# Mixing the tokens of each pair of heads in the space of the keys

## The chip, the core and the metric

The kernel runs on one core of a Trainium2 chip. A core has five engines with an instruction stream of their own: PE (TensorE, which multiplies matrices; its weight loads are listed apart as PEld), DVE (VectorE), ACT (ScalarE), POOL (GpSimd) and SP (SyncE, which issues the DMA transfers here). Engines wait for one another by semaphores. SBUF is the working memory of 128 partitions, PSUM the memory of eight banks into which PE writes. The metric is device time in microseconds; the shown runs of one kernel lie within 0.15% of one another, and this document calls a difference of under 0.2% (3.6 us) no change.

## The reference

Cut to what matters: an attention whose keys and values are averaged over 8 neighbouring tokens (576 tokens, 72 keys), a mixing of the tokens by two low-rank matrices U (576 x 32) and V (32 x 576), and two large feed-forward layers.

```python
# q, k, v: 8 batches, 8 heads, 576 tokens, 64 features
k_p = k.reshape(B, H, Sp, pool, D).mean(axis=3)      # 72 keys
v_p = v.reshape(B, H, Sp, pool, D).mean(axis=3)
scores = scale * q @ k_p.T;  attn = softmax(scores)   # 576 x 72 for each head
x = attn @ v_p                                        # then 8 x 576 x 512
h = x.transpose(0, 2, 1) @ U @ V                      # mixes the 576 tokens
u = x + h.transpose(0, 2, 1)
x = u + relu(u @ w_ch1) @ w_ch2                       # layer 1: 512 -> 2048 -> 512
# layer 2: layer norm, the same form, another pair of weights
```

## The kernel before, in words

Weights arrive as 64-bit floats and are decoded on the chip by integer operations on DVE (lines 564 to 593). Most products are made of two 32-bit pieces in the reduced format fp32r, a high part and the rest (`split`, line 519), so that one product of the reference becomes three matmuls: high by high, rest by high, high by rest. A few small ones are made in full fp32; the trace lists each of those as two records.

The attention runs over 32 pairs of heads, four pairs to a batch (`att_steps`, line 1019). For a pair P: load q, k, v; sum keys and values over 8 tokens (`att_prep`); scores of all 576 tokens against 2 x 72 keys, in five row tiles of 128 tokens, the last one overlapping (`att_s`, five fp32 matmuls of 144 columns); minimum, exponential, sum and division (`att_m`), which leaves the tile `sc` [128 tokens, 5, 144]; transposes of `sc` to key by token (`att_t`, eight of 128 tokens and two of 64); the product with the values (`att_av`), which leaves `xT` [128 features, 576 tokens].

Before the change, the four `xT` of a batch are then mixed at its end: `att_xt` transposes them back to token by feature (20 transposes), splits them (in the first two batches with an extra matmul against a negative identity, `split_ps`, line 533), `att_g` multiplies with U (ten matmuls of 512 columns; U stands in `ust` with its pieces side by side), `att_gs` cuts the product into pieces (`gs`), `att_vm` multiplies with V (eight matmuls of 288 columns) and adds to `xT` on DVE. Then `a_split` (first batch) or a trip through DRAM (`u_d`, `a_prep`) gives layer 1 its input.

Layer 1 runs in groups of 512 tokens (`a_l1`, 12 matmuls of 512 columns for each of 8 slices of weights, then `a_l2`). The group w-1 of layer 1 is interleaved with the attention of batch w, so that PE has its matmuls to do while the attention waits. The first batch has no such partner.

The order is made by a planner in the kernel file (`Order.schedule`, line 151): every operation has a cost for each engine that may do it, a priority that grows with the PE cost of what was written before it (shifted by biases), and buffers from rings; the planner gives each operation to an engine and emits each engine's stream in order of planned start. An engine then works its stream strictly in that order. The PSUM ring of the attention, `py`, has four banks handed out in turn.

The names and lines that the steps touch: `att_t` 849, `att_xt` 931, `att_g` 949, `att_gs` 961, `att_vm` 975, the order of steps 1028 to 1053, `setup_uv` (decodes U and V) 609, its place 1128.

Of the kernel before, what the change touches and what calls it, by code (L numbers as in the profile page):

```python
# [8 lines left out]
F32 = mybir.dt.float32  # L9
# [28 lines left out]
UT = [0, 128, 256, 384, 512]  # L38
# [363 lines left out]
class Kern:  # L402
    def __init__(self, nc, tc, aps):
# [129 lines left out]
    def split_ps(self, hi, lo, ps, src, n, m):  # L533

        nc, o = self.nc, self.o
        on = {ACT: c_act(n, True), DVE: c_dve(n)}
        part = lambda: src(ps.t)
        o.op({ACT: on[ACT]}, lambda e: copy(nc, e, hi(), part()), r=[ps], w=[hi.a])
        o.op(
            {PE: c_pe(n)},  # L540
            lambda e: e.matmul(part(), self.minus[:m, :m], hi(), start=False, stop=True, skip_group_check=True),
            r=[hi.a],
            w=[ps],
        )
        o.op(on, lambda e: copy(nc, e, lo(), part()), r=[ps], w=[lo.a])

# [62 lines left out]
    def setup_uv(self):  # L609
# [4 lines left out]
        def load(raw):  # L614
            o.op(
                {GP: 200},
                lambda e: e.memset(raw.t[64:, 4 * RANK : n].bitcast(I32), 0),
# [11 lines left out]
            o.op({SY: 450}, lambda e: e.dma_start(raw.t[:64, 4 * RANK : n], self.U[512:]), w=[(raw, 1)], size=16384)  # L629
# [5 lines left out]

        for c in (0, 1, 3):
# [14 lines left out]
        for z in range(2):  # L651
# [11 lines left out]
            x = self.staged(SH, load)  # L663
# [185 lines left out]
    def att_t(self, P, j):  # L849
# [24 lines left out]
        o.op({PE: cost}, mm, r=[sc], w=[ps])  # L874
        if P < LEAN_T:
# [55 lines left out]
    def att_xt(self, b, i):  # L931
        o = self.o
        n = 128 if i < 4 else 64
        ps, xh, xl = self.buf("py"), self.buf("xh"), self.buf("xl")
        xs = [self.xT[NP * b + p] for p in range(NP)]

        def mm(e):
            for p in range(NP):
                turn(e, ps.t[:n, p * 128 : p * 128 + 128], xs[p].t[:, UT[i] : UT[i] + n], self.ident, p == 0)

        o.op({PE: 4 * 110}, mm, r=xs, w=[ps])
        top = lambda t: t[:n]
        if NP * b < LEAN_X:
            self.split_ps(View(xh, None, top), View(xl, None, top), ps, top, DM, n)
        else:
            self.split(View(xh, None, top), View(xl, None, top), View(ps, None, top), DM, ps=True, hi_on=(ACT,))
        self.xhl[i] = (xh, xl, n)

    def att_g(self, b, i):
        if i == 0:  # L950
            self.pg = self.buf("py")
        pg = self.pg
        xh, xl, n = self.xhl[i]

        def mm(e):
            e.matmul(pg.t, self.ust.t[:n, i], xh.t[:n], start=(i == 0), stop=False)  # L956
            e.matmul(pg.t, self.ust.t[:n, i], xl.t[:n], start=False, stop=(i == 4))  # L957

        self.o.op({PE: c_pe(DM, 2)}, mm, r=[xh, xl, self.ust], w=[pg])

    def att_gs(self, b):
        nc, o = self.nc, self.o
        gr, gs, pg = self.buf("gr"), self.buf("gs"), self.pg
        o.op({ACT: c_act(DM, True)}, lambda e: copy(nc, e, gr.t, pg.t), r=[pg], w=[gr])
        o.op(
            {DVE: c_dve(DM) + 60},
# [697 lines left out]
```

## Time and profile before

| | us |
|---|---|
| median of 3 runs (lowest, highest) | 1775.42 (1773.33, 1775.81) |
| the profiled execution | 1774.35 |
| its span in the trace | 1772.6 |
| PE busy | 1738.5 (98%) |
| DVE busy | 973.2 (55%) |
| POOL, ACT busy | 745.9 (42%), 723.8 (41%) |

The span is what the trace covers; 1.75 us lie around it. Busy shares are means over stages that differ: up to about 93 us the attention of the first batch and the start of the second, then layer 1 interleaved with the other batches up to about 475 us, the rest of layer 1 to about 620 us, and layer 2.

### The profile page before, as it was taken

To read this page: it belongs to the slowest core of one execution; us is meant where nothing else is said; L and a number is where in the kernel's file an instruction comes from. 1 tells how busy PE (TensorE), PEld (TensorE's weight loads), DVE (VectorE), ACT (ScalarE), POOL (GpSimd) and SP (SyncE) were. 2 spreads that over 40 slices of the span, in tenths; PEclk is the share of its full clock that TensorE was granted. 3 is DMA by queue.
4 is the path that set the end of the run, shared out by engine and by line. 5 is a ranking of instruction groups with operands and counts; after the bars stand their busy time and mean duration, and the time that the engine had idled before them with its cause. 6 is when DMAs were issued, how large, how long until landed. Compare 5 with 4: busy or idle time off the path is not lost.

```text
span 1772.6 us, 26907 instructions
## 1 busy us (share of the span) xinstructions
PE 1738.5 (98%) x10156; PEld 1519.6 (86%) x10156; DVE 973.2 (55%) x1858; ACT 723.8 (41%) x1897; POOL 745.9 (42%) x638
## 2 busy tenths in 40 slices
PE   5899999999999999999999999999999999999998
PEld 4678888888888889999999988999999999899997
DVE  8998888888646354444445766553224633333333
ACT  5556556655632233333333443333333433223221
POOL 1233224222100066666666653333334455555654
PEclk8799999999999999999999999999999999999999
DMA  6555544654343153544444444332112423233222
GB/s 194 179 165 181 189 162 155 206 182 132 108 141 112 42 196 123 123 120 122 121 120 106 132 130 157 119 122 81 48 48 84 143 101 102 102 114 112 102 78 78
DMA packets 95251, 222.97 MB, mean 126 GB/s; under 512 B 14225, under 2 KB 14225, under 8 KB 89361
## 3 DMA queue, kind: packets, MB, share of 16 engines
q1 hardware_dynamic: 94976, 221.25, 39.4%
q8 instruction: 79, 1.29, 0.3%
q14 instruction: 52, 0.42, 0.1%
q10 hardware_dynamic: 144, 0.00, 0.0%
HBM read 152.00 MB, written 69.22 MB: 125 GB/s over the span
## 4 chain that ended last, share of the span: by engine, by line
PE 94%; DVE 4%; DMA 1%; ACT 0%; issue 0%; DVEq 0%; ACTq 0%
PE py L1387 33%; PE pa L1299 17%; PE pbc L1299 13%; PE pbc L1097 11%; PE pa L1069 10%; PE py L378 3%; PE py L792 2%; PE py L918 1%; PE py L919 1%; PE py L900 1%; PE py L956 1%; PE py L957 0%; PE py L981 0%; PE pbc L1522 0%; DMA wraw<-w_d 0%
## 5 line engine op out<-in xcount | busy, mean ns | idle before, releaser
L1387 PE MATMUL py<-hid,w2h 128*128 128x512 f32 x1728 | 541.2, 394 | 0.2 <-DVE hid L1327 0.2
L1387 PE MATMUL py<-hid,w2l 128*128 128x512 f32 x864 | 338.6, 392 | 0.0
L1299 PE MATMUL pa<-op,w1h 128*128 128x256 f32 x1728 | 326.2, 281 | 0.5 <-ACT s L383 0.3
L1299 PEld LDWEIGHTS pa<-op,w1h 128*128 128x128 f32 x1728 | 293.9, 188 | 37.0 <-DVE s L385 0.6
L528 POOL TENSOR_TENSOR op<-xraw,op 128x512 fp32r<-128x512 f32 x130 | 171.5, 1321 | 280.2 <-ACT op L383 275.7
L1357 DVE TENSOR_TENSOR pbc<-s,pbc 128x512 f32<-128x512 f32 x108 | 75.1, 696 | 390.2 <-PE pbc L1299 386.0
L1387 PEld LDWEIGHTS py<-hid,w2h 128*128 128x128 f32 x1728 | 273.5, 189 | 11.0 <-DVE hid L1327 0.5
L1299 PEld LDWEIGHTS pbc<-op,w1h 128*128 128x128 f32 x1296 | 220.7, 188 | 28.1
L1299 PE MATMUL pbc<-op,w1h 128*128 128x256 f32 x1296 | 244.3, 281 | 0.0
L1299 PE MATMUL pa<-op,w1l 128*128 128x256 f32 x864 | 242.6, 281 | 0.0
L1387 PEld LDWEIGHTS py<-hid,w2l 128*128 128x128 f32 x864 | 162.4, 188 | 36.7
L1097 PE MATMUL pbc<-op,wh 128*128 128x512 f32 x576 | 183.7, 400 | 0.0
L1069 PE MATMUL pa<-hid,wh 128*128 128x512 f32 x576 | 181.9, 397 | 0.0
L1299 PE MATMUL pbc<-op,w1l 128*128 128x256 f32 x648 | 181.8, 280 | 0.0
L1299 PEld LDWEIGHTS pa<-op,w1l 128*128 128x128 f32 x864 | 162.9, 189 | 0.0
L1327 DVE SCALAR_TENSOR_TENSOR hid<-pa,hid 128x512 fp32r<-128x512 f32 x108 | 74.5, 690 | 123.8 <-ACT hid L1321 123.6
L1321 ACT ACTIVATE hid<-pa 128x512 fp32r<-128x512 f32 x108 | 64.6, 598 | 188.5 <-PE pa L1299 184.2
L1321 ACT ACTIVATE hid<-pbc 128x512 fp32r<-128x512 f32 x108 | 64.6, 598 | 184.9 <-DVE pbc L1357 183.9
L1253 POOL TENSOR_TENSOR t<-xraw 128x512 f32<-128x512 f32 x52 | 67.8, 1303 | 138.3 <-DMA xraw<-n_d 80.8
L1069 PEld LDWEIGHTS pa<-hid,wh 128*128 128x128 f32 x576 | 104.9, 188 | 20.9 <-issue 0.4
L1299 PEld LDWEIGHTS pbc<-op,w1l 128*128 128x128 f32 x648 | 121.9, 188 | 0.0
L1097 PEld LDWEIGHTS pbc<-op,wh 128*128 128x128 f32 x576 | 103.1, 188 | 20.8 <-issue 2.2
(187 smaller groups left out, 2896.0 us busy)
## 6 DMA issues: line engine op xcount, KB each, us to landing
xraw<-n_d SPq DMA_DIRECT2D x18, 1024.0 KB
wraw<-wC SPq DMA_DIRECT2D x32, 512.0 KB
wraw<-wA SPq DMA_DIRECT2D x24, 512.0 KB
w_d<-wx SPq DMA_DIRECT2D x48, 256.0 KB
wraw<-w_d SPq DMA_DIRECT2D x48, 256.0 KB
k<-kT SPq DMA_DIRECT2D x32, 288.0 KB
q<-qT SPq DMA_DIRECT2D x32, 288.0 KB
v<-v SPq DMA_DIRECT2D x32, 288.0 KB
```

The costliest lines, as they stand in the source:

```text
L378: e.matmul(out, src, ident, start=first, stop=True, is_transpose=True, skip_group_check=True)
L528: lambda e: e.tensor_sub(lo(), src(), hi().bitcast(F32)),
L792: lambda e: e.matmul(ps.t[:, i : i + 2 * SP], q.t[:, QT[t] : QT[t] + 128], kbd.t.rearrange("p h n -> p (h n)"), start=True, stop=True, ski ...
L900: lambda e: e.matmul(ps.t[:, :SH], vs.t[:, w], ef.t[:, h, c], start=(h == 0), stop=(h == 1)),
L1069: e.matmul(ps.t, w.t[:, c], u.t, start=(i == 0), stop=(i == 3 * NCC - 1))
L1097: e.matmul(ps.t, w.t[:, c], x.t, start=(f == 0 and j == 0), stop=(f == NA - 1 and j == 2))
L1253: o.op(on, lambda e: e.tensor_sub(dst(), a(), c()), r=r, w=w)
L1299: e.matmul(bank.t[:, sl], w.t[:, self.WCOL[k], c], u.t[:, t], start=(first and i == 0), stop=(last and i == 5), skip_group_check=True,)
L1321: lambda e: e.activation(h.t[:, :TG], bank.t, AF.Relu),
L1327: lambda e: e.scalar_tensor_tensor(l.t[:, :TG], bank.t, 0.0, h.t[:, :TG].bitcast(F32), op0=ALU.max, op1=ALU.subtract),
L1357: o.op({DVE: c_dve(TG)}, lambda e: e.tensor_add(c.t, s.t, c.t), r=[s], w=[c])
L1387: e.matmul(y.t, w.t[:, i, c], x.t[:, :TG], start=(first and q == 0), stop=(last and q == 2))
```

## The change

The mixing is linear in the softmax weights, so the kernel applies U and V to them and not to the attention's result. For each pair, `att_u` multiplies the softmax weights (144 columns) with U; for pairs 0 to 7 in fp32 with a plain copy of U (`us`), for the others with the split pieces (`sh`, `sl`) in ten matmuls. `gs` is now 144 columns for a pair. `att_t` transposes `sc` as before and then adds `gs` times V into the same PSUM banks: two matmuls of 512 columns and two of 64. The evicted weights are the mixed ones; `att_av` then gives the mixed `xT` at once, and `att_out` stores it. `att_xt`, `att_g`, `att_vm` and `split_ps` are gone, all pairs have the same order of steps, and U and V are decoded right after the first pair's preparation (`first`), not in the middle of the first batch.

```diff
-        ring(att, "xT", [128, S], n=5)
-        ring(att, "xh", [128, DM], F32R, 2)
-        ring(att, "xl", [128, DM], F32R, 2)
-        ring(att, "gr", [128, DM], F32R)
-        ring(att, "gs", [128, DM], F32R)
+        ring(att, "xT", [128, S], n=3)
+        ring(att, "sh", [128, 5, 2 * SP], F32R)
+        ring(att, "sl", [128, 5, 2 * SP], F32R)
+        ring(att, "gr", [128, 2 * SP], F32R, 2)
+        ring(att, "gs", [128, 2 * SP], F32R, 2)
...
+        ring(att, "us", [128, 5, 128])
...
+        self.us = self.buf("us")
+        o.op({GP: 500}, lambda e: e.memset(self.us.t, 0.0), w=[self.us])
+        for c in (0, 1, 3):
...
+        gs = self.gs[P]
+        parts = [(j, slice(0, 512), slice(0, 512))] if j < 2 else [
+            (h, slice(h * 64, h * 64 + 64), slice(512, S)) for h in range(2)
+        ]
+
+        def add(e):
+            for h, a, k in parts:
+                e.matmul(
+                    ps.t[:SP, a], gs.t[:, h * SP : h * SP + SP], self.vst.t[:, k], start=False, stop=True,
+                    skip_group_check=True,
+                )
+
+        o.op({PE: c_pe(512) if j < 2 else 2 * 65}, add, r=[gs, self.vst], w=[ps])
...
+    def att_u(self, P):
+        nc, o = self.nc, self.o
+        sc, ps = self.sc[P], self.buf("py")
+        row = lambda t: slice(64 if t == 4 else 0, 128)
+        if P < LEAN_U:
+
+            def mm(e):
+                for t in range(5):
+                    r = row(t)
+                    e.matmul(ps.t[:, : 2 * SP], self.us.t[r, t], sc.t[r, t], start=(t == 0), stop=(t == 4))
+
+            o.op({PE: 5 * 200}, mm, r=[sc, self.us], w=[ps])
         else:
...
+            h, l = self.buf("sh"), self.buf("sl")
+            whole = lambda t: t
+            self.split(View(h, None, whole), View(l, None, whole), View(sc, None, whole), 10 * SP)
+
+            def mm(e):
+                for t in range(5):
+                    r = row(t)
+                    e.matmul(ps.t[:, : 2 * SP], self.ust.t[r, t], h.t[r, t], start=(t == 0), stop=False)
+                    e.matmul(ps.t[:, : 2 * SP], self.ust.t[r, t], l.t[r, t], start=False, stop=(t == 4))
+
+            o.op({PE: 10 * 75}, mm, r=[h, l, self.ust], w=[ps])
+        gr, gs = self.buf("gr"), self.buf("gs")
+        o.op({ACT: c_act(2 * SP, True)}, lambda e: copy(nc, e, gr.t, ps.t[:, : 2 * SP]), r=[ps], w=[gr])
...
-        first += [m(0)]
+        first += [m(0), lambda: self.att_u(0)]
...
-                seq += [M_, x[0], x[1], g[0], x[2], R_[0], g[1], x[3], g[2], x[4], g[3], g[4], gs]
-                seq += vm
+            seq = [S_[0], R_[2], S_[1], T_[0], S_[2], S_[3], T_[1], S_[4], T_[2], R_[1], M_, V_[0]]
+            seq += [V_[1], R_[0], V_[2], V_[3], out, U_]
```

Where the planner puts it shows at two places of the PE stream and one of the DVE stream. In the rows a name with its buffer number stands left of the arrow for what is written and right of it for what is read.

The first place is the PE stream from the end of the first batch's mixing to the first matmuls of layer 1 (`pa0<-hid0,wh00`). Before, first half of that stretch and its end:

```order
L981 MATMUL py3_249<-vstk0_189,gs0_187 128x288
L981 MATMUL py2_248<-vstk0_189,gs0_187 128x288
L981 MATMUL py0_246<-vstk0_189,gs0_187 128x288
L981 MATMUL py1_247<-vstk0_189,gs0_187 128x288
L792 MATMUL py3_249<-kbd1_154,q1_156 128x144 x2
L378 MATMUL py2_248<-ident_60,sc0_167 72x128 x4
L792 MATMUL py3_249<-kbd1_154,q1_156 128x144
L792 MATMUL py0_246<-kbd1_154,q1_156 128x144
L378 MATMUL py1_247<-ident_60,sc0_167 72x128 x4
L792 MATMUL py0_246<-kbd1_154,q1_156 128x144
L378 MATMUL py2_248<-ident_60,sc0_167 72x64 x2
L1069 MATMUL pa0_242<-hid0_209,wh00_220 128x512
```

Now, the same stretch, with the fifth pair's product with U (`py<-sc,us`), scores (`kbd,q`), transposes (`ident,sc`) and additions (`vstk,gs`):

```order
L948 MATMUL py1_246<-sc0_167,us0_187 128x144 x5
L787 MATMUL py3_248<-kbd1_154,q1_156 128x144 x2
L377 MATMUL py2_247<-ident_60,sc0_167 72x128 x4
L877 MATMUL py2_247<-vstk0_188,gs0_184 72x512
L787 MATMUL py3_248<-kbd1_154,q1_156 128x144
L787 MATMUL py0_245<-kbd1_154,q1_156 128x144
L377 MATMUL py1_246<-ident_60,sc0_167 72x128 x4
L877 MATMUL py1_246<-vstk0_188,gs0_184 72x512
L787 MATMUL py0_245<-kbd1_154,q1_156 128x144
L377 MATMUL py2_247<-ident_60,sc0_167 72x64 x2
L877 MATMUL py2_247<-vstk0_188,gs0_184 72x64 x2
L1049 MATMUL pa0_241<-hid0_208,wh00_219 128x512
```

The products of the batch's mixing (`vstk0,gs0` of 288 columns, and before them the transposes of `xT` and the products with `ust`) no longer stand ahead of layer 1; three additions of the fifth pair stand there, and layer 1 begins behind them.

The second place is the PE stream in the stretch where layer 1 and attention are interleaved. Before, the third batch's four products with V behind layer 1's matmuls (`pbc0<-op14,wh70`):

```order
L1097 MATMUL pbc0_244<-op14_207,wh70_234 128x512
L1097 MATMUL pbc0_244<-op15_208,wh70_234 128x512
L1097 MATMUL pbc0_244<-op14_207,wl70_235 128x512
L981 MATMUL py2_248<-vstk0_189,gs0_187 128x288
L981 MATMUL py0_246<-vstk0_189,gs0_187 128x288
L981 MATMUL py3_249<-vstk0_189,gs0_187 128x288
L981 MATMUL py1_247<-vstk0_189,gs0_187 128x288
L1097 MATMUL pbc1_245<-op0_193,wh00_220 128x512
```

Now the ninth pair's last products with U (`sh`, `sl`: high and rest of the softmax weights), then the tenth pair's scores, the ninth's transposes and first addition:

```order
L959 MATMUL py3_248<-sh0_180,ust0_186 128x144
L960 MATMUL py3_248<-sl0_181,ust0_186 128x144
L959 MATMUL py3_248<-sh0_180,ust0_186 128x144
L960 MATMUL py3_248<-sl0_181,ust0_186 128x144
L787 MATMUL py0_245<-kbd1_154,q1_156 128x144 x2
L377 MATMUL py2_247<-ident_60,sc0_167 72x128 x4
L787 MATMUL py0_245<-kbd1_154,q1_156 128x144
L787 MATMUL py1_246<-kbd1_154,q1_156 128x144
L877 MATMUL py2_247<-vstk0_188,gs0_184 72x512
L377 MATMUL py3_248<-ident_60,sc0_167 72x128 x4
L1077 MATMUL pbc0_243<-op8_200,wh40_227 128x512
```

Ten short products for each pair have come into the stream, each with a weight load of its own, and the first addition follows them behind five short groups.

The third place is the DVE stream just ahead of layer 1's first matmuls. Before, the pieces `gs0` of the first batch and the additions to `xT`:

```order
L593 SCALAR_TENSOR_TENSOR wx0_145<-wraw0_144,wx0_145 128x512
L967 SCALAR_TENSOR_TENSOR gs0_187<-gr0_186,neg_b_72,py1_247 128x512
L528 TENSOR_TENSOR wl40_229<-wx0_145,wh40_228 128x512
L988 TENSOR_TENSOR xT0_177<-xT0_177,py3_249 128x288
L988 TENSOR_TENSOR xT0_177<-xT0_177,py2_248 128x288
L988 TENSOR_TENSOR xT1_178<-xT1_178,py0_246 128x288
L385 CAST hid0_209<-xT0_177 128x512
L988 TENSOR_TENSOR xT1_178<-xT1_178,py1_247 128x288
L988 TENSOR_TENSOR xT2_179<-xT2_179,py3_249 128x288
L988 TENSOR_TENSOR xT2_179<-xT2_179,py2_248 128x288
L988 TENSOR_TENSOR xT3_180<-xT3_180,py0_246 128x288
```

Now the splits of the fourth pair's result (`hid6`, `hid7`), decoding (`wx0`, `at0`, `wt0`) and the fifth pair's `gs0`:

```order
L833 RECIPROCAL sm0_171<-sm0_171 128x10
L384 CAST hid6_214<-xT0_177 128x512
L837 TENSOR_TENSOR sc0_167<-sc0_167,sm0_171 128x720
L528 TENSOR_TENSOR hid7_215<-xT0_177,hid6_214 128x512
L564 TENSOR_SCALAR wt0_146<-wt0_146 128x512
L528 TENSOR_TENSOR wl00_220<-ax0_151,wh00_219 128x512
L571 SCALAR_TENSOR_TENSOR wx0_145<-wraw0_144,wt0_146 128x512
L579 SCALAR_TENSOR_TENSOR wx0_145<-wraw0_144,wx0_145 128x512
L554 TENSOR_SCALAR at0_152<-araw0_150 128x512
L967 SCALAR_TENSOR_TENSOR gs0_184<-gr0_182,neg_b_72,py1_246 128x144
```

The eight additions to `xT` are gone from DVE; splits that POOL and ACT made before, a piece `gs` for each pair and more of the weights' decoding stand in their place.

## Rows read from the trace of the kernel before

**Rows 1.** The page, part 1: engine, busy us (share), instructions.

```profile
PE 1738.5 (98%) x10156; PEld 1519.6 (86%) x10156; DVE 973.2 (55%) x1858; ACT 723.8 (41%) x1897; POOL 745.9 (42%) x638
```

**Rows 2.** Busy time by stretch: us, then each engine, PEclk, DMA.

```profile
0.00:20.00 20.00, 9.30 (x38) 7.72 (x39) 14.23 (x36) 10.36 (x49) 4.63 (x20) 1.00 0.67 210
20.00:48.00 28.00, 20.33 (x83) 15.17 (x83) 23.96 (x60) 15.52 (x71) 4.35 (x4) 0.69 0.58 182
48.00:72.00 24.00, 18.41 (x68) 13.49 (x67) 22.07 (x44) 12.72 (x31) 5.45 (x6) 0.65 0.54 186
72.00:93.00 21.00, 18.15 (x95) 14.53 (x94) 20.66 (x45) 13.72 (x64) 5.85 (x7) 1.00 0.47 147
93.00:475.00 382.00, 381.19 (x2013) 316.34 (x2012) 317.49 (x677) 229.85 (x824) 108.92 (x122) 1.00 0.53 170
...
620.00:1772.00 1152.00, 1146.09 (x7195) 1032.27 (x7194) 505.61 (x870) 398.35 (x775) 610.87 (x475) 1.00 0.36 111
```

**Rows 3.** Timeline of PE, first batch's mixing: start us, us, operation, count.

```profile
48.89 1.91 PE L378 MATMUL py<-ident,xT 128*128 128x128 f32 x8
...
60.24 0.50 PE L957 MATMUL py<-xl,ust 64*128 64x512 f32 x1 [0.43 <-ACT xl L383]
64.24 3.19 PE L981 MATMUL py<-vstk,gs 128*128 128x288 f32 x8 [3.50 <-DVE gs L967]
...
71.76 0.73 PE L1069 MATMUL pa<-hid,wh 128*128 128x512 f32 x2
```

**Rows 4.** Groups of DVE by form, 0 to 72 us: busy, mean ns.

```profile
L842 DVE TENSOR_TENSOR sc<-sc,sm 128x720 f32<-128x720 f32 x5 | 4.5, 900 | 0.0
...
L988 DVE TENSOR_TENSOR xT<-xT,py 128x288 f32<-128x288 f32 x8 | 3.1, 446 | 0.0
...
L967 DVE SCALAR_TENSOR_TENSOR gs<-gr,neg_b,py 128x512 fp32r<-128x512 f32 x1 | 0.7, 740 | 0.0
```

**Rows 5.** Timeline of PE in the third batch's mixing, saturated stretch.

```profile
173.22 1.03 PE L378 MATMUL py<-ident,xT 128*128 128x128 f32 x8
174.01 0.72 PE L1069 MATMUL pa<-hid,wh 128*128 128x512 f32 x2
174.57 0.40 PE L1069 MATMUL pa<-hid,wl 128*128 128x512 f32 x1
...
185.29 0.39 PE L1097 MATMUL pbc<-op,wl 128*128 128x512 f32 x1
185.61 0.50 PE L956 MATMUL py<-xh,ust 64*128 64x512 f32 x1
185.94 0.39 PE L957 MATMUL py<-xl,ust 64*128 64x512 f32 x1
186.27 0.73 PE L1097 MATMUL pbc<-op,wh 128*128 128x512 f32 x2
186.83 0.40 PE L1097 MATMUL pbc<-op,wl 128*128 128x512 f32 x1
...
189.12 0.68 PE L981 MATMUL py<-vstk,gs 128*128 128x288 f32 x4
189.64 0.63 PE L1097 MATMUL pbc<-op,wh 128*128 128x512 f32 x2
190.11 0.39 PE L1097 MATMUL pbc<-op,wl 128*128 128x512 f32 x1
```

**Rows 6.** Timeline of PE, the score products of the same stretch.

```profile
200.71 0.90 PE L792 MATMUL py<-kbd,q 128*128 128x144 f32 x6
201.35 0.73 PE L1097 MATMUL pbc<-op,wh 128*128 128x512 f32 x2
201.92 0.40 PE L1097 MATMUL pbc<-op,wl 128*128 128x512 f32 x1
```

**Rows 7.** Timeline of PE, products of one column, in the second layer.

```profile
697.34 0.95 PE L1522 MATMUL pbc<-few,lns 128*128 128x1 f32 x8
698.15 0.48 PE L1299 MATMUL pa<-op,w1h 128*128 128x256 f32 x2
```

More of the change, by code (lines that the diff above doesn't have):

```diff
@@ L531, in split @@
         )
[L533 to L545, printed above, removed]
     def decode(self, x, tmp, raw):
@@ L634, in u @@
             return t[:, :n].rearrange("p (i r) -> p i r", r=RANK)
+        self.us = self.buf("us")
+        o.op({GP: 500}, lambda e: e.memset(self.us.t, 0.0), w=[self.us])
+        for c in (0, 1, 3):
+            o.op(
+                {ACT: c_act(n), DVE: c_fast(n)},
+                lambda e, c=c: copy(nc, e, self.us.t[:, :, c * RANK : (c + 1) * RANK], u(x.t)),
+                r=[x],
+                w=[(self.us, c)],
+            )
         for c in (0, 1, 3):
@@ L661, in load @@
                     )
-            x = self.staged(SH, load)
+            x = self.staged(SH, load, 'aw'[z])
             o.op(
@@ L965, in att_gs @@
         o.op(
-            {DVE: c_dve(DM) + 60},
+            {DVE: c_dve(2 * SP) + 60},
             lambda e: e.scalar_tensor_tensor(
-                gs.t, gr.t.bitcast(F32), self.neg_b, pg.t, op0=ALU.mult, op1=ALU.add
+                gs.t, gr.t.bitcast(F32), self.neg_b, ps.t[:, : 2 * SP], op0=ALU.mult, op1=ALU.add
             ),
-            r=[gr, pg],
+            r=[gr, ps],
             w=[gs],
         )
-        self.gs = gs
-    def att_vm(self, b, half, c):
+        self.gs[P] = gs
@@ L976, in att_vm, with att_out @@
+    def att_out(self, P):
         o = self.o
-        x, gs, ps = self.xT[NP * b + c], self.gs, self.buf("py")
-        s = slice(half * SH, half * SH + SH)
-        o.op(
-            {PE: c_pe(SH)},
-            lambda e: e.matmul(
-                ps.t[:, :SH], gs.t[:, c * 128 : c * 128 + 128], self.vst.t[:, s], start=True, stop=True
-            ),
-            r=[gs, self.vst],
-            w=[ps],
-        )
-        keys = [(x, (h, half)) for h in range(2)]
-        o.op({DVE: c_dve(SH)}, lambda e: e.tensor_add(x.t[:, s], x.t[:, s], ps.t[:, :SH]), r=[ps], w=keys)
@@ L1028, in att_steps @@
         pv = lambda P: (lambda: self.att_prep_v(P))
-        first = [ld(0), pr(0), pv(0), ld(1)] + [s(0, t) for t in range(5)] + [pr(1), pv(1), ld(2)]
-        first += [m(0)]
+        first = [ld(0), pr(0), self.setup_uv, pv(0), ld(1)] + [s(0, t) for t in range(5)] + [pr(1), pv(1), ld(2)]
+        first += [m(0), lambda: self.att_u(0)]
         for P in range(B * NP):
             N = P + 1
-            last = P % NP == NP - 1
             S_ = [s(N, t) for t in range(5)] if N < B * NP else [None] * 5
             M_ = m(N) if N < B * NP else None
+            U_ = (lambda N=N: self.att_u(N)) if N < B * NP else None
             R_ = [ld(P + 3), pr(P + 2), pv(P + 2)] if P + 2 < B * NP else [None] * 3
@@ L1038, in att_steps @@
             V_ = [av(P, 0, 0), av(P, 1, 0), av(P, 0, 1), av(P, 1, 1)]
[L1039 to L1050 removed]
+            out = lambda P=P: self.att_out(P)
+            seq = [S_[0], R_[2], S_[1], T_[0], S_[2], S_[3], T_[1], S_[4], T_[2], R_[1], M_, V_[0]]
+            seq += [V_[1], R_[0], V_[2], V_[3], out, U_]
             if P == 0:
@@ L1127, in phase_a @@
         per = self.att_steps()
[L1128 to L1131 removed]
+        for st in per[0]:
             st()
```

72 lines of the change are left out of this document (15 added, 57 removed).

## The prediction

> **What bounds the kernel now.** I read the page's busy shares first: PE is busy for 98% of the span, no other engine for more than 55% [rows 1]. That is a mean, so next the busy time by stretch [rows 2]. From 93 to 475 us, where layer 1 and the attention are interleaved, PE is busy 381.2 of 382 us at a granted clock of 1.00: there every microsecond of PE work that is added or taken is a microsecond of the kernel. DVE has 64 us to spare in that stretch and ACT 152. The first 72 us are another matter: PE idles 5 to 11 us in each of three stretches, its clock is 0.69 and 0.65 of full speed in two of them (a mix of the 1.2 and 2.4 GHz levels, after idle gaps), and DVE is busy 60.3 of 72 us, 46.0 of the last 52. Third, the timeline of PE around the first batch's mixing [rows 3]: the transposes back begin at 48.89, the last product with U at 60.24, PE then waits 3.50 us for `gs`, multiplies with V at 64.24, and layer 1 begins at 71.76. So the change touches two things with different prices: the amount of PE work where PE is the bound, and the time at which layer 1 can begin.
>
> **PE work in the saturated stretch, taken away.** The third batch shows what a mixing costs there [rows 5]. Two products of 512 columns take 190.11 - 189.64 = 0.47 us, so 0.23 each. Eight transposes and two such products lie between 173.22 and 174.57: 1.35 - 0.46 = 0.89, so 0.11 for a transpose and 2.2 for twenty. The ten products with U are 2.3 us, and the last two of them, on 64 rows, cost more: from 185.52 (0.23 behind the start at 185.29) to 186.37 (0.46 ahead of 186.83) it is 0.85 us where two products elsewhere take 0.46. So a visit to 64 rows costs 0.39 extra, and U 2.7 in all. The four products with V take 190.11 - 0.46 - 189.12 = 0.53 us, so 0.13 each and 1.05 for eight. A batch's mixing is 2.2 + 2.7 + 1.05 = 5.95 us of PE. Seven batches lie behind the start of layer 1: 41.65, and the second batch has five products with the negative identity besides, 5 x 0.23 = 1.15. Taken away: 42.8 us.
>
> **PE work added.** At the start of layer 1 the fifth pair's additions are done (the order shows it), so 27 pairs are left. Each adds two products of 512 columns (0.46) and two of 64. The latter are not in the trace; products of one column take (698.15 - 697.34) / 8 = 0.10 each [rows 7], and I take that: 0.66 a pair, 17.8 us. Three pairs have the product with U in fp32, 144 columns with 128 x 128 weights, which is the form of the scores: six records take 201.92 - 0.46 - 200.71 = 0.75 us [rows 6], 0.125 a record, two records each: 5 x 0.25 and 0.39 for the last tile, which is on 64 rows: 1.64, three times 4.9 us.
>
> For 24 pairs it is ten fp32r products of 144 columns, each with its own weight load, and the trace has none of that form. From below: half of a product of 288 columns, 0.065 us, if time goes by columns alone. From above: a record of the scores, same columns and same weights, 0.125. The one-column rows decide between them: a product with almost nothing to stream still takes 0.10, and the transposes of 128 columns 0.11, both with a load of 128 x 128 weights for each. So the load sets the pace of short products, and I take 0.11. Eight of them are 0.88; the two on 64 rows, 0.39 and twice 0.065; together 1.40 us, 33.6 for 24 pairs. Added: 17.8 + 4.9 + 33.6 = 56.3, less 42.8 taken away: **+13.5 us**. Bounds: with 0.065, no charge for 64 rows and 0.03 for 64 columns, 33.4 - 42.8 = -9.4; with 0.125 for all short products, 60.6 - 42.8 = +17.8.
>
> The Trainium skill (TensorE: Matmul & The Clock Gate, section Back-to-back issue gap) gives a warm product N / 2.4 GHz and 2.5 ns more, which is 0.0625 us for 144 columns; its section on LDWEIGHTS lets a load go by the columns of the weights, 107 ns for 128. By the first rule the eight products of a pair would be 0.38 us cheaper and the sum 9 us lower, 1777; by the second it stays. Rows 7 agree with the second: 0.10 us for a product of one column.
>
> **The start of layer 1.** Removed is the chain from 48.89 to 64.24 and the products with V. But in PE's new order layer 1 still stands behind the fifth pair's transposes and now its additions too, which need that pair's `gs` from DVE. So I ask when DVE gets there. In its order it has 138 instructions ahead of that point before and 146 now. Gone are eight additions (3.1 us) and one `gs` (0.7) [rows 4]; new are five short `gs` (0.3 each as an estimate between half of the old one, 0.37, and less than an addition of 288 columns, 0.45), two copies of U, and splits, copies and decoding that ACT, POOL or a later time had before. At the mean of the first 72 us (60.3 us for 140 instructions, 0.43) eight more would be 3.4 us; as many of the new ones are short I take 1.4. Against this, DVE idled 11.7 us, of which 5.8 lie in the first 20 us, where the first loads and scores are waited for; of the other 6 some fell to waits for a cold PE that the long chain brought, and half of it may go. Together the first matmul of layer 1 comes 2 us earlier, at about 70. Bounds: 8 earlier if all idle time behind the first 20 us and the added work go, 4 later if DVE keeps its idle time and has the 3.4.
>
> **What I cost at nothing.** The splits of the softmax weights (720 columns; the nearest row has 0.90 on DVE [rows 4]) and four short `gs` a batch: at most 4 x (0.90 + 0.90 + 0.45) = 9 us a batch against 8 x 0.446 + 0.74 and five splits that go; DVE's 64 us of idle time in 93 to 475 hide the difference, and if that cover were gone the splits would delay U and so PE. The stores of `xT` go out one by one and not four together; SP waits for them in turn, with the loads of the next pairs behind, but three buffers of `xT` cover a pair. A new wait is that of the first addition for `gs`, through ACT and DVE; behind it on PE stand the scores of the next pair and layer 1's matmuls. In the order five short groups cover it (0.25 x 4 and four transposes, about 1.4 us, against one copy and one piece of 144 columns). I take 0, with 5 us as bound for all pairs. Layer 2 and the rest of layer 1 keep their matmuls.
>
> **Sum.** +13.5 - 2 = +11.5 us on the profiled execution's own 1774.35 (span 1772.6 and 1.75 around it): 1786 us. That execution lies 1.1 us under the median of the runs shown, which is less than the 0.2% (3.6 us) that I call no change.
>
> **Rivals.**
> 1. *The start is what counts (faster).* PE needs 22.9 us from 48.89 to 71.76, and the fourth pair is done at 48.9. If layer 1 could start some 3 us behind it, at 52, that is -20, and with +13.5 the time is 1768. The point from which it decides is a start before 54.7 (71.8 - 13.5 - 3.6). For it: PE idled and was slow there. Against it: DVE's 46.0 of 52 us, and that little of its work goes. Chance 0.12.
> 2. *Short products go by columns.* Then the term is -9.4 and the time 1763; if only the 144 columns are cheap and the 64 rows cost what they did, it is +4.9 and 1777. Against it stand the one-column rows. The skill's rule on the gap, above, is this rival. Chance 0.10.
> 3. *The additions wait.* `gr` stands in ACT's stream among the exponentials, `gs` in DVE's among long splits. If each of 27 pairs holds PE for 0.5 us (about one more DVE instruction of 0.45), it is 13.5 more: 1799. For it: PE works strictly in order, and there are four such waits a batch where there was one. Against it: PE's idle time in 93 to 475 was 0.8 us, with waits of this kind in it. Chance 0.12.
>
> **How the numbers follow.** The forecast has 0.66, with a range of its own from 1777 (start 8 earlier, short products at 0.10) to 1794 (start 4 later, 4 of the waits). Of it 0.56 is slower by over 0.2%, that is above 1779, and 0.10 within. Rival 3 is slower in full. Rival 1 gives 0.09 faster and 0.03 same; rival 2 gives 0.06 faster and 0.04 same, as half of it ends at 1777. Faster 0.15, same 0.17, slower 0.68. The range for 8 in 10 reaches down into the first two rivals and up to the third: 1769 to 1798.
>
> **What would show it.** In the changed profile: the ten products of a pair taking 1.3 to 1.5 us (0.7 would be rival 2); PE busy nearly all of the interleaved stretch, but that stretch some 10 us longer; the first matmul of layer 1 between 64 and 76 us (under 55 would be rival 1); idle time of PE ahead of the additions of 512 columns under 5 us in total (13 would be rival 3); DVE still over 85% busy from 20 us to the start of layer 1. I am wrong if the interleaved stretch gets shorter, or if the start moves by more than 10 us.

## The result, and the profile after

The changed kernel takes 1787.92 us (median of 4 runs, 1787.38 to 1788.03) where the kernel before takes 1774.86 beside it (4 runs, 1773.33 to 1775.81): a ratio of 1.0075, 95% interval 1.0063 to 1.0087. That is 13.1 us slower; forecast were 11.5. The profiled execution's span grew by 12.7 us, from 1772.6 to 1785.3. First the busy time of the engines over the whole span, the answer to [rows 1]:

```profile
PE 1750.8 (98%) x10290; PEld 1536.5 (86%) x10290; DVE 969.0 (54%) x1853; ACT 702.0 (39%) x1874; POOL 733.5 (41%) x612
```

PE has 12.3 us more busy time, DVE 4.2 less. Next the same stretches as in [rows 2] (us, then busy time of PE, PEld, DVE, ACT, POOL, granted clock, DMA share, GB/s):

```profile
0.00:20.00 20.00, 6.35 (x23) 5.51 (x24) 13.59 (x40) 6.20 (x27) 3.39 (x19) 1.00 0.74 206
20.00:48.00 28.00, 21.05 (x88) 16.14 (x88) 25.95 (x56) 11.68 (x52) 8.21 (x9) 0.79 0.56 174
48.00:72.00 24.00, 16.70 (x76) 13.47 (x74) 21.84 (x48) 11.06 (x50) 5.20 (x6) 0.78 0.55 171
72.00:93.00 21.00, 21.00 (x105) 17.36 (x103) 16.95 (x39) 10.63 (x49) 6.37 (x7) 0.87 0.58 190
93.00:475.00 382.00, 381.80 (x2064) 320.12 (x2062) 312.26 (x668) 214.64 (x800) 92.41 (x91) 1.00 0.54 169
620.00:1772.00 1152.00, 1151.37 (x7228) 1037.40 (x7227) 504.65 (x870) 402.66 (x782) 610.58 (x475) 1.00 0.36 111
```

PE is still full from 72 us on (in the first 5 us of that at half clock). All of the difference lies ahead of layer 2, as its first matmul in the timelines of PE shows, of before and of after:

```profile
617.00 0.40 PE L1299 MATMUL pa<-op,w1h 128*128 128x256 f32 x2
```

```profile
630.00 0.40 PE L1276 MATMUL pa<-op,w1h 128*128 128x256 f32 x2
```

It comes 13.0 us later; behind it both kernels take 1155.5 us (1772.6 - 617.0 and 1785.3 - 630.0 are 0.3 apart). So the time up to that matmul can be divided. The start, in PE's timeline of the changed kernel (start, us, operation, count, idle time ahead and what ended it):

```profile
4.98 2.74 PE L787 MATMUL py<-kbd,q 128*128 128x144 f32 x10 [4.98 <-DVE kbd L391]
...
43.72 3.03 PE L948 MATMUL py<-sc,us 128*128 128x144 f32 x10 [3.94 <-DVE sc L837]
...
58.11 3.03 PE L948 MATMUL py<-sc,us 128*128 128x144 f32 x10 [4.30 <-DVE sc L837]
...
70.78 3.03 PE L948 MATMUL py<-sc,us 128*128 128x144 f32 x10 [2.99 <-DVE sc L837]
...
78.61 0.70 PE L1049 MATMUL pa<-hid,wh 128*128 128x512 f32 x2
```

Layer 1 begins at 78.61 and not at 71.76 [rows 3], 6.85 us later, where I had said 2 earlier. Every pair of the first batch, and the fifth, now has a product with U behind the norm of the softmax on DVE (`sc`). Four of the five wait for it and then run at half clock: 3.03 us for ten records, where the same ten take 1.66 at full clock (e8_fifth_later, below). The second pair's, at 31.32, has no such wait.

But the start of layer 1 is a poor measure, because work can move past it. A better one divides the whole time up to layer 2 into PE's idle time, the loss by the clock (half of the busy time in periods at the lower of its two levels, 1.2 and 2.4 GHz), and the rest, which is work at full clock. The clock's column reads 1.00 in the first 20 us, but the ten score products at 4.98 take 0.27 us each: the records of the clock begin only at 22.7 us (16.8 in before), and I count what lies ahead of them as half clock too. In us, each row from one profiled execution, which lies up to 1.9 us from the median of its kernel; kernels that do the same work differ by up to 2 us in the last column (before, e1, e11: 571.5 to 573.6), so the account is good to about that:

| kernel | layer 1 begins | layer 2 begins | idle | clock | lost | work |
|---|---|---|---|---|---|---|
| before | 71.8 | 617.0 | 27.6 | 16.9 | 44.5 | 572.5 |
| after | 78.6 | 630.0 | 28.1 | 17.0 | 45.1 | 584.9 |
| e1_early_uv | 75.0 | 614.4 | 25.1 | 17.8 | 42.9 | 571.5 |
| e2_first_old | 70.9 | 627.2 | 22.3 | 20.9 | 43.2 | 584.0 |
| e3_first_new | 70.3 | 613.5 | 28.4 | 12.2 | 40.6 | 572.9 |
| e4_high_only | 77.9 | 620.3 | 31.4 | 18.0 | 49.4 | 570.9 |
| e5_full_rows | 76.6 | 619.5 | 31.2 | 12.5 | 43.8 | 575.7 |
| e6_wide | 79.2 | 622.4 | 29.2 | 16.5 | 45.7 | 576.7 |
| e7_both | 75.4 | 609.6 | 29.7 | 13.8 | 43.5 | 566.1 |
| e8_fifth_later | 67.4 | 631.0 | 30.4 | 15.7 | 46.1 | 584.8 |
| e10_short_decode | 61.9 | 619.9 | 23.7 | 10.9 | 34.6 | 585.3 |
| e11_before_short | 71.5 | 611.6 | 21.7 | 16.4 | 38.0 | 573.6 |
| e12_no_additions | 79.2 | 618.3 | 30.2 | 17.2 | 47.5 | 570.8 |

The idle times can be followed in the windows: 13.65 + 6.95 + 7.30 = 27.9 for the changed kernel up to 93 us. By this account the change costs +12.4 us of work and +0.6 of lost time: the total is work. (The expectations below call the loss 40.5 and 41.3; those are the same sums without the stretch ahead of the clock's first record.)

What the work is made of, in the saturated stretch of the changed kernel: a pair's product with U, start by start, and a pair's last addition:

```profile
142.06 0.23 PE L959 MATMUL py<-sh,ust 128*128 128x144 f32 x1
142.12 0.27 PE L960 MATMUL py<-sl,ust 128*128 128x144 f32 x1
142.24 0.28 PE L959 MATMUL py<-sh,ust 128*128 128x144 f32 x1
142.35 0.27 PE L960 MATMUL py<-sl,ust 128*128 128x144 f32 x1
...
142.69 0.28 PE L959 MATMUL py<-sh,ust 128*128 128x144 f32 x1
142.80 0.27 PE L960 MATMUL py<-sl,ust 128*128 128x144 f32 x1
143.00 0.33 PE L959 MATMUL py<-sh,ust 64*128 64x144 f32 x1
143.17 0.27 PE L960 MATMUL py<-sl,ust 64*128 64x144 f32 x1
143.37 0.76 PE L787 MATMUL py<-kbd,q 128*128 128x144 f32 x4
143.97 0.60 PE L377 MATMUL py<-ident,sc 128*72 128x128 f32 x4
...
149.14 0.32 PE L877 MATMUL py<-vstk,gs 128*72 128x64 f32 x2
149.29 0.71 PE L1077 MATMUL pbc<-op,wh 128*128 128x512 f32 x2
```

From the second product on the starts are 0.11 us apart, around the two products on 64 rows 0.20, 0.17 and 0.20; the ten take 143.37 - 142.06 = 1.31 us here and 1.32 in the mean of 24 pairs. Two additions of 64 columns take 0.15.

### The profile page after: what moved, and what is told of

Its sections match the earlier page's. It is cut to its first block, busy times and chain, and to the rows that moved or that the text cites. A ratio compares the mean times of both kernels' runs of the same rounds, so it can differ in the third digit from the quotient of the medians.

```text
span 1785.3 us, 27080 instructions
## 1 busy us (share of the span) xinstructions
PE 1750.8 (98%) x10290; PEld 1536.5 (86%) x10290; DVE 969.0 (54%) x1853; ACT 702.0 (39%) x1874; POOL 733.5 (41%) x612
## 3 DMA queue, kind: packets, MB, share of 16 engines
q8 instruction: 80, 1.31, 0.3%
## 4 chain that ended last, share of the span: by engine, by line
PE 96%; DVE 2%; DMA 1%; ACT 0%; issue 0%; SPq 0%; DVEq 0%; ACTq 0%
PE py L1364 33%; PE pa L1276 17%; PE pbc L1276 13%; PE pa L1049 11%; PE pbc L1077 11%; PE py L787 2%; PE py L377 2%; PE py L877 1%; PE py L948 1%; PE py L959 1%; PE py L908 1%; PE py L960 1%; PE py L926 1%; PE py L927 1%; DMA wraw<-wA 1%; PE pbc L1499 0%
## 5 line engine op out<-in xcount | busy, mean ns | idle before, releaser
L1364 PEld LDWEIGHTS py<-hid,w2h 128*128 128x128 f32 x1728 | 273.5, 189 | 10.9 <-DVE hid L1304 0.5
L1276 PEld LDWEIGHTS pbc<-op,w1h 128*128 128x128 f32 x1296 | 220.7, 188 | 28.1
```

The source lines that it names most:

```text
L1276: e.matmul(bank.t[:, sl], w.t[:, self.WCOL[k], c], u.t[:, t], start=(first and i == 0), stop=(last and i == 5), skip_group_check=True,)
L1364: e.matmul(y.t, w.t[:, i, c], x.t[:, :TG], start=(first and q == 0), stop=(last and q == 2))
```

## The experiments

Each was timed beside the kernel before; differences in us are taken from the ratio, whose interval is about 1 to 1.5 thousandths to either side, some 2 to 3 us.

**e1_early_uv: the place of U and V alone, in the kernel before.** The two halves of V are also decoded through two sets of buffers, as in the changed kernel.

```diff
-            x = self.staged(SH, load)
+            x = self.staged(SH, load, 'aw'[z])
...
-        first = [ld(0), pr(0), pv(0), ld(1)] + ...
+        first = [ld(0), pr(0), self.setup_uv, pv(0), ld(1)] + ...
```

> The kernel before (mixing batch by batch), with one edit: the load and decoding of U and V stands where the changed kernel has it, right behind the first pair's preparation, instead of in the middle of the first batch. Theory A (what stands early in DVE's list sets the start: decoding U and V ahead of the first norm pushes the rest back): the first norm at about 15.3 us instead of 12.3, the first matmul of layer 1 at 74 to 76 us instead of 71.8, the time +1 to +4 us over before (ratio 1.0005 to 1.0025). Rival B (the serial round softmax, U, gs, additions of each pair makes the start late, not the decoding): the start stays within 1 us of 71.8 and the time within 0.05% of before.

Ratio 0.9984 (0.9974 to 0.9993): 2.8 us faster; the interval is clear of 1, though the difference is under the 0.2% that this document calls no change. Layer 1 did begin later, at 75.0, as theory A has it, and the time did not get longer. The planner put a pair's products with the values and six score records more ahead of that start, and lost time fell by 1.6 us. Neither theory holds for the time, and the start of layer 1 is no measure of it.

**e2_first_old and e3_first_new: the change in one part of the batches.** U and V go with the first batch: e2 decodes them where before does, e3 where the changed kernel does, so e3 has the edit of e1 in it.

```diff
+PAIRWISE = range(1, B)        # e2; (0,) in e3
...
-        gs = self.gs[P]
+        if P // NP in PAIRWISE:
+            gs = self.gs[P]
...
+            if b in PAIRWISE or P % NP < NP - 1:
```

> A mix of both kernels: the first batch is mixed as before (one mixing for four pairs, behind them), batches two to eight pair by pair as in the changed kernel. Theory: two separate terms. The start is back at 71 to 73 us, and only the PE work of the interleaved stretch is left, which I read as +9.5 us from the two traces (56.3 added, 40.6 taken away, less some 6 that other groups lost); one more pair with an fp32 product falls into the stretch: +9 to +13 us over before, 1784 to 1787. Rival (the later start costs the whole of the loss and the interleaved stretch itself is even): +1 to +4 us.

Ratio 1.0059 (1.0044 to 1.0074): 10.5 us slower, with 11.5 us more work and 1.3 less lost. As the theory said: nearly the whole loss is PE work in batches two to eight.

> The other mix: only the first batch is mixed pair by pair, batches two to eight as before. Theory: the first matmul of layer 1 comes at 77 to 80 us as in the changed kernel, the 3 us of PE idle time that before has right behind its start are gone, PE work behind it is that of before: +2.5 to +5 us over before, 1777 to 1780. Rival (the start costs its full 6.9 us, since the idle time behind it comes from elsewhere): +6 to +8. Rival (the start is not worth anything, layer 2 is waited for by something else): 0.

Ratio 0.9976 (0.9967 to 0.9985): 4.3 us faster, which none of my three lines had. Layer 1 began at 70.3 and not at 77 to 80. Work is even (572.9 against 572.5), and 3.8 us less are lost: the clock's part falls from 16.9 to 12.2. How much of that is the missing chain of transposes back, U, `gs` and V at the end of the batch is not shown, since the earlier U and V of e1 alone gave 2.8 us; the intervals of the two overlap.

The two parts don't add up to the whole: +10.5 and -4.3 make +6.2, where the changed kernel has +13.1. Work does add up (11.5 and 0.4, against 12.4); lost time does not (-1.3 and -3.8, against +0.6). So the changed kernel gives back what each mix won. Likely, but not isolated: in it the fifth pair has its product with U ahead of layer 1 too, waits 2.99 us for it (at 70.78, above) and runs it at half clock.

**e8_fifth_later: the fifth pair behind layer 1's first matmuls.**

```diff
-A_BIAS = -40000.0
+A_BIAS = -32000.0
```

> The changed kernel with one number of the planner: the attention's lead over layer 1 is 32 us instead of 40 in its own reckoning, which puts the first group of layer 1's matmuls ahead of the fifth pair's product with U and its additions on PE. The work is the same. Theory (the fifth pair's U and additions, run after a wait and at half clock, are what the changed kernel loses at the start): layer 1 begins at 66 to 70 us instead of 78.6, the 3.0 us wait and the 3.4 us of half clock of that pair go, in part or whole: 3 to 6 us below the changed kernel, 1782 to 1785. Rival (what sets the start is DVE's list, in which the splits of xT and of layer 1's weights stand no earlier): the first matmuls of layer 1 wait for hid or wl instead, no change within 1.5 us. Rival (other waits later in the stretch come from the shorter lead): slower.

Ratio 1.0083 (1.0068 to 1.0098): 14.7 us slower than before, 1.6 more than the changed kernel, which is no change. Layer 1 began at 67.4, 11 us earlier, and it was worth nothing. The timeline of PE:

```profile
67.41 0.85 PE L1049 MATMUL pa<-hid,wh 128*128 128x512 f32 x2
...
71.35 1.66 PE L948 MATMUL py<-sc,us 128*128 128x144 f32 x10 [0.18 <-DVE sc L837]
...
79.75 1.07 PE L377 MATMUL py<-ident,sc 128*72 128x128 f32 x4 [4.88 <-DVE gs L967]
```

The product with U no longer waits, but the additions behind it now do, 4.88 us for `gs`, and the clock is at half once more from 77.0 to 83.8. The theory failed and what the third line says came out: the wait moved to a later place.

**e10_short_decode and e11_before_short: less work for DVE.**

```diff
+        if short:                                             # layer 1's weights
+            self.o.op(
+                {DVE: c_fast(n)},
+                lambda e: e.tensor_scalar(
+                    x.t[:, :n].bitcast(I32), raw.t[:, :n].bitcast(I32).rearrange("p (n two) -> p n two", two=2)[:, :, 1],
+                    0x3FFFFFFF, None, op0=ALU.bitwise_and,
+                ),
+                r=[raw],
+                w=[x],
+            )
+            return x
         self.decode(xv, View(tmp, None, lambda t: t[:, :n]), View(raw, None, lambda t: t[:, :n]))
```

> The changed kernel with the decoding of layer 1's weights cut from five DVE or ACT instructions per half to one (layer 1 then works on numbers that aren't the weights; all its other instructions stay). About four DVE instructions and 2.2 us of DVE go for each of the eight or nine halves that are decoded before layer 1 begins, 18 us of DVE's 67 there. I read the start by the PE time lost before layer 2 (idle time, and half of the busy time at half clock): 40.5 us in the changed kernel. Theory (DVE's list sets the pace of the first 78 us): 8 to 15 us of the loss go, 1773 to 1780. Rival (the serial round of each pair, scores, minimum, exponentials, norm, U, gs, additions, sets the pace, with DVE merely busy beside it): the loss stays within 3 us of 40.5 and the time within 3 us of 1788.

Ratio 1.0021 (1.0012 to 1.0031): 3.7 us over before, so 9.4 below the changed kernel, at 1779.0. Lost time falls by 10.5 us and work stays. (The planner, given the cheaper decoding, also put layer 1 ahead of the fifth pair's product with U; by e8_fifth_later that gains nothing by itself.) The windows of this kernel, as above, and PE's products with U:

```profile
0.00:20.00 20.00, 6.27 (x22) 5.43 (x23) 13.51 (x40) 6.11 (x27) 3.39 (x19) 1.00 0.77 215
20.00:48.00 28.00, 22.27 (x102) 17.63 (x101) 23.08 (x54) 11.21 (x52) 2.96 (x3) 0.82 0.73 242
48.00:72.00 24.00, 19.73 (x102) 15.45 (x102) 21.22 (x48) 11.76 (x56) 2.18 (x3) 0.93 0.72 225
```

```profile
16.47 3.04 PE L961 MATMUL py<-sc,us 128*128 128x144 f32 x10 [8.71 <-DVE sc L850]
...
29.65 2.87 PE L961 MATMUL py<-sc,us 128*128 128x144 f32 x10 [1.43 <-DVE sc L850]
41.44 3.04 PE L961 MATMUL py<-sc,us 128*128 128x144 f32 x10 [3.00 <-DVE sc L850]
53.61 2.87 PE L961 MATMUL py<-sc,us 128*128 128x144 f32 x10 [2.41 <-DVE sc L850]
61.93 0.84 PE L1062 MATMUL pa<-hid,wh 128*128 128x512 f32 x2
65.56 1.66 PE L961 MATMUL py<-sc,us 128*128 128x144 f32 x10 [0.43 <-DVE sc L850]
```

So DVE's list does set part of the start: 10 of the 45 us lost go with it. But both theories have a share. From the first product with U to the fifth it is 65.56 - 16.47 = 49.1 us, 12.3 a pair; in the changed kernel 70.78 - 16.39 = 54.4, 13.6 a pair. Up to the fifth product DVE is busy 51.5 us instead of 60.2, and four pairs gain only 5.3 us. What is left of a round is mostly the serial chain. In the round from 41.44 to 53.61 the product with U holds PE to 44.40, where the next pair's scores begin; ACT's exponentials end at 51.10, and DVE, busy with other work, begins that pair's division at 52.11. So DVE's queue accounts for 1.0 of the round's 12.2 us at that point.

> The kernel before with the same cut of layer 1's decoding. Its loss before layer 2 is 41.3 us. Theory (DVE's list sets the pace there too): 8 to 15 us go, 1760 to 1767. Rival (the chain of the first batch's mixing sets the end of that stretch): at most 4 us go, 1771 or more.

Ratio 0.9958 (0.9944 to 0.9972): 7.5 us faster, 1767.5, just above the theory's bracket and below the rival's. Lost time falls by 6.5 us. The kernel before is held by DVE too; by one execution of each, less than the changed one (6.5 against 10.5).

**e4_high_only, e12_no_additions: the two added pieces of work, priced by leaving them out.**

```diff
-                    e.matmul(ps.t[:, : 2 * SP], self.ust.t[r, t], h.t[r, t], start=(t == 0), stop=False)
-                    e.matmul(ps.t[:, : 2 * SP], self.ust.t[r, t], l.t[r, t], start=False, stop=(t == 4))
+                    e.matmul(ps.t[:, : 2 * SP], self.ust.t[r, t], h.t[r, t], start=(t == 0), stop=(t == 4))
```

> The changed kernel without the products of U with the low parts of the softmax weights (five fp32r products of 144 columns instead of ten in 24 pairs; that part of the sum is left out, the split on ACT, DVE and POOL stays). Theory (each short product costs its 0.11 us, PE is the bound): 24 x 5 x 0.111 = 13.3 us less, and the visit to 64 rows, one product shorter, up to 24 x 0.2 = 4.8 less: 1770 to 1775. Rival (short products by their 144 columns, 0.065): 7.8 less, 1780. Rival (the waits for splits and gs set the pace of a pair): no change, 1788.

Ratio 1.0025 (1.0014 to 1.0036): 8.7 us below the changed kernel, 1778.8, outside the theory's bracket. By the time alone the rival with the columns (1780) would be the nearer one. The five products that are left, and the scores behind them, decide against it:

```profile
140.75 0.83 PE L959 MATMUL py<-sh,ust 128*128 128x144 f32 x5
141.50 0.76 PE L787 MATMUL py<-kbd,q 128*128 128x144 f32 x4
```

0.75 us where ten took 1.31, so 0.56 for five, 0.112 each and not 0.065; all work falls by 14.1 us, 0.59 a pair. The time falls by less because 4.3 us more are lost, which none of the three lines had: PE now waits for `gs` later in the interleaved stretch, 93 to 620 us (us in total, times, longest):

```profile
PE py L877 <- DVE gs L966: 2.3, 1, 2.3
PE py L377 <- DVE gs L966: 0.9, 1, 0.9
```

and one of these gaps is followed by a period at half clock (1.7 us of loss).

```diff
-        o.op({PE: c_pe(512) if j < 2 else 2 * 65}, add, r=[gs, self.vst], w=[ps])
+        if P < LEAN_U:
+            o.op({PE: c_pe(512) if j < 2 else 2 * 65}, add, r=[gs, self.vst], w=[ps])
```

> The changed kernel without the additions of pairs nine to 32 (the mixing of these pairs is left out of the result; the products with U, gr and gs stay). Theory (an addition of 512 columns costs 0.23 us, the two of 64 columns 0.15 together, and nothing waits for gs): 24 x 0.60 = 14.5 us less than the changed kernel, 1773. By the prediction's 0.66 a pair it would be 15.8, 1772. Rival (the additions hide part of what the transposes ahead of them take): 24 x 0.45 = 11 less, 1777. Rival (PE also waits for gs there, each pair by 0.2 us or more): 19 less, 1769.

Ratio 0.9993 (0.9984 to 1.0003): 14.3 us below the changed kernel, 1774.3. Work falls by 14.1 us, 0.59 for a pair's additions, as the first line said. By the time alone the 15.8 of the prediction's 0.66 can't be told from it, and in the profiled execution 2.4 us more are lost, 1.4 of them in one wait for `gs`.

**e5_full_rows, e6_wide, e7_both: the product with U made cheaper.** The fifth tile of U has 64 rows of zeros, so the product can run on all 128; and the two parts of the weights can lie side by side, so that U is loaded five times and not ten.

```diff
-        row = lambda t: slice(64 if t == 4 else 0, 128)
+        row = lambda t: slice(0, 128)                         # e5, e7
```

```diff
-        ring(att, "sh", [128, 5, 2 * SP], F32R)
-        ring(att, "sl", [128, 5, 2 * SP], F32R)
+        ring(att, "shl", [128, 5, 2, 2 * SP], F32R)           # e6, e7
+        ring(att, "su", [128, 2 * SP])
...
+                    e.matmul(ps.t[:, : 4 * SP], self.ust.t[r, t],
+                        hl.t[r, t].rearrange("p a n -> p (a n)"), start=(t == 0), stop=(t == 4))
...
+                lambda e: e.tensor_reduce(su.t, ps.t[:, : 4 * SP].rearrange("p (a n) -> p n a", a=2), axis=AX.X, op=ALU.add)
```

> The changed kernel with the fifth tile's product with U on all 128 rows (the upper 64 rows of that tile of U are zeros) instead of on 64 rows, in all 32 pairs. Theory (the visit to 64 rows is what those products pay for): a pair's ten fp32r products take 10 x 0.111 = 1.11 us instead of 1.33, 24 x 0.22 = 5.3 less; the fp32 pairs 5 x 0.25 instead of 1.51, 8 x 0.26 = 2.1 less; 7.4 us below the changed kernel, 1780 to 1782, ratio to before 1.003 to 1.004. Rival (the last products of a group pay for the change to another kind of product, whatever their rows): no change, 1788.

Ratio 1.0005 (0.9996 to 1.0014): 12.2 us below the changed kernel, more than I expected. Work falls by 9.2 us. A pair's ten products, first and last start, and the scores behind them:

```profile
138.44 0.23 PE L959 MATMUL py<-sh,ust 128*128 128x144 f32 x1
...
139.41 0.27 PE L960 MATMUL py<-sl,ust 128*128 128x144 f32 x1
139.51 0.70 PE L787 MATMUL py<-kbd,q 128*128 128x144 f32 x4
140.05 0.60 PE L377 MATMUL py<-ident,sc 128*72 128x128 f32 x4
```

1.07 us instead of 1.31, and the four scores behind them 0.54 instead of 0.60 in the same place (the transposes stand at 143.97 above): the visit to 64 rows was paid by the products behind it as well. Work fell by more than the expected 7.4, and the time by 3.0 more than the work: 1.3 is lost time, the rest lies within the intervals. The rival is refuted: it had no change.

> The changed kernel with high and low parts of the softmax weights side by side: five fp32r products of 288 columns instead of ten of 144 in 24 pairs, the halves added by one more DVE instruction before gr and gs. Same columns, half the weight loads. Theory (the load sets the pace of a short product: 0.11 for 144 columns, and 288 columns take 0.13): 5 x 0.13 and 0.3 for the visit to 64 rows, 0.95 instead of 1.33 a pair, 9 us below the changed kernel, 1778 to 1780. Rival (columns count alone): the same PE work, no gain, 1788. Rival (the added DVE instruction makes the additions wait for gs): the PE work falls as said, but idle time of PE ahead of the additions of 5 us or more takes half of it or all back, 1783 to 1788.

Ratio 1.0034 (1.0022 to 1.0046): 7.0 us below the changed kernel, at 1780.8 just above the expected 1778 to 1780; work falls by 8.2 us. Five products of 288 columns and the scores behind them:

```profile
142.23 1.02 PE L960 MATMUL py<-shl,ust 128*128 128x288 f32 x5
143.18 0.76 PE L787 MATMUL py<-kbd,q 128*128 128x144 f32 x4
```

0.95 us as expected, for the same columns that took 1.31 with twice the loads. Columns alone are refuted as the price. PE waited for `gs` once in the stretch, 0.5 us. The edit halves the products along with the loads, so it does not by itself tell a load from a fixed cost of each product. Two things speak for the load: the additions of 64 columns, whose weights have 72 columns and not 128, take 0.07 each, below 0.11, and in the changed kernel's trace a weight load's own record is 0.143 us long for these 72 columns and 0.188 for the 128 of layer 1's products. No run changes the width of the weights alone.

> Both edits together: five products of 288 columns on all 128 rows. Theory: 5 x 0.13 = 0.65 us a pair instead of 1.33, 24 x 0.68 = 16.3 and the 2.1 of the fp32 pairs: 18 us below the changed kernel, 1769 to 1771, ratio to before 0.997 to 0.998. If the two gains come from the same place (the 64-row visit is nothing but two more loads), only 12 less: 1776.

Ratio 0.9966 (0.9954 to 0.9979): 1767.9 us, 19.1 below the changed kernel and 6.0 below the one before. The same place:

```profile
136.85 0.83 PE L960 MATMUL py<-shl,ust 128*128 128x288 f32 x5
137.52 0.65 PE L787 MATMUL py<-kbd,q 128*128 128x144 f32 x4
```

0.67 us a pair, half of the changed kernel's. In PE work, mixing pair by pair beats mixing by batch as it stands once U costs that: 566.1 us against 572.5. In time the case is less clear. e7_both has the lowest ratio of the kernels here that do all of the work, but the intervals of e3_first_new and of e1_early_uv, which still mixes by batch, overlap with it. And the mixing by batch has a visit to 64 rows too, 0.39 us a batch by the prediction's rows, some 3 us in all by that estimate, which no run takes out.

## Why the prediction came out near, and which steps failed

- **What bounds the kernel.** Right: from 72 us on PE is full, and the experiments that took PE work away there moved the time by about that much (e6, e7 and e12 within 1.2 us; e4 by 5.4 less, of which 4.3 came back as lost time; e5 by 3.0 more).
- **PE work taken away, 42.8.** 40.6 by the starts of the products in the kernel before: the transposes back cost 13.65 / 140 = 0.098 each and not 0.11; the ten products with U 18.26 / 7 = 2.6 and not 2.7; those with V 0.131, as said.
- **PE work added, 56.3.** 52.2: the additions 0.59 a pair and not 0.66, by leaving them out (e12_no_additions), 16.0 for 27 pairs; three fp32 products 4.5 (4.9 said); the fp32r products 31.7, 1.32 a pair (1.40 said). From start to start the additions take more, 19.8, but a transpose ahead of one hands over to it after 0.028 us where two transposes are 0.109 apart, so part of that is the transposes' own time. The choice that decided, 0.11 for a short product from the one-column rows [rows 7], is what the timeline shows and what e4_high_only and e6_wide confirm. The transposes, which the prediction took as its second witness for the load, say nothing of it: within a group those of `sc`, with weights of 72 columns, take the same 0.109 from start to start as those of `xT` with 128. The Trainium skill (TensorE: Matmul & The Clock Gate, section Back-to-back issue gap) has 0.0625 us by its formula, which it gives for a product by itself, and some 81 ns at 128 columns for a stream with loads. The trace has 0.11 at full clock, above both. The same page's section on LDWEIGHTS has 107 ns for 128 columns, by its formula. The pace agrees with that; the records of such loads, 0.188 us long, do not.
- **The net, +13.5.** With these prices it is +11.6. Measured behind the start are +6.15 (551.39 against 545.24 from the first matmul of layer 1 to layer 2): +9.6 of work, and -3.5 of idle time that before has just behind its start (2.85 us in [rows 2], 0.8 later). So the term was 7.4 us too large: 1.9 by its own prices, 3.5 by idle time that it did not count, and 2.0 by the pace of products that it put at nothing ("Layer 2 and the rest of layer 1 keep their matmuls"). They are kept, but layer 1's take 3.3 us less in all; of those of the second half each takes 0.2334 us and not 0.2366 (864 of them, 2.8 us). The products with the values take 2.2 less, scores and transposes some 3.4 more. Why layer 1's run closer isn't tested by a run; fewer changes to another kind of product among them would be a reason.
- **The start of layer 1, -2.** This step failed: "Together the first matmul of layer 1 comes 2 us earlier, at about 70". It came 6.85 later, outside the bound of 4. I counted DVE's instructions, and took PE's waits there for a consequence of the old chain that would half go. Instead each pair got a link more in its serial round, the product with U behind the norm. Up to 93 us PE's waits for norms, first before and then after (us in total, times, longest), are:

```profile
PE py L378 <- DVE sc L842: 6.9, 4, 2.9
PE py L948 <- DVE sc L837: 19.9, 4, 8.7
```

  Waits of before for other things went in exchange, the 3.5 us for the batch's `gs` among them, so idle time up to layer 2 is 28.1 against 27.6.

- **Luck in the total.** In the prediction's own terms the start was 8.85 us off one way and the work behind it 7.35 the other, and the total came out within 1.6. Part of that is one thing on two sides of a line: 2.8 us more work stand ahead of the start (the mixing of five pairs instead of one of a batch), and the idle time behind it moved ahead of it. Up to layer 2 the two terms are +12.4 of work and +0.6 of lost time, where +13.5 and -2 were said: errors of 1.1 and 2.6 that still have opposite signs. That the slowdown is work in the batches two to eight was foreseen and is shown (e2_first_old); that the sum met 13.1 so closely was not earned.
- **What I cost at nothing.** For waits right in the changed kernel: PE waits 0.2 us for splits and never for `gs` behind the start. The cover is thin, as e4, e8 and e12 show: with PE work gone, or a pair moved, waits of 1.4 to 4.9 us for `gs` appear at once.
- **The rivals.** The start as the thing that counts: an early start was worth nothing in e8_fifth_later, and what the first batch's part gave in e3_first_new is 4.3 us and not 20, with e1's 2.8 in it. Short products by columns: refuted. Additions that wait: not in the changed kernel behind the start.
- **What would show it.** Ten products of 1.3 to 1.5 us: 1.31. DVE over 85% busy from 20 us to the start: 53.0 of 58.6, 90%. The interleaved stretch "some 10 us longer": 6 by the clock, 9.6 of work. The start "between 64 and 76": missed.

## What to carry to other kernels

Don't price a short matmul by its columns alone. Here each cost about the same 0.11 us down to one column, and more beside products on 64 rows: put pieces that share weights side by side, and pad a part tile to full rows when zeros are free. When work is traded between stages, add up idle time, time at half clock and work up to a common point, since a milestone such as the first matmul of a stage moves with what the scheduler puts ahead of it. Moving work out of the way of a serial chain only moved the wait here (e8); taking work off the engine that holds it shortened it (e10), as far as the chain's own length allowed. Before calling a difference the effect of one edit, look what else the kernel took over with it (e3 has e1's edit in it).

## What I had not expected of the hardware

- A visit of two products to 64 of the 128 rows costs more than their own time: 0.20, 0.17 and 0.20 us between starts instead of 0.11, and some 0.06 more at the next four; all 32 pairs on full rows took 9.2 us of work less.
- Doubling the columns of a product from 144 to 288 took its pace only from 0.11 to 0.134 us a product, on full rows (e5_full_rows, e7_both).
- The clock's record in a profile begins late: up to 20 us the windows show 1.00, while the products run at the pace of the lower level (0.27 us for 144 columns, against 0.125 at full clock).
- The order alone can be worth some 3 us: e1_early_uv does the work of before and is 0.16% faster (interval 0.07 to 0.26%).
